# A two-layer squared-ReLU MLP: smaller first loads, a shorter warm-up and a reordered tail

## The chip, the cores and the metric

The kernel runs on one core of a Trainium2 chip. The metric is device time in microseconds (us), the median of several executions. The kernel before was measured again beside each set of experiments, on the same chip. The profile's span is counted from its first to its last instruction and is about 1.7 us shorter than the measured time.

## The reference, cut to what matters

```python
B, S, D, F = 1, 2048, 640, 1536           # bf16 everywhere
h = jnp.einsum("bsd,df->bsf", x, w1) + b1
r = jnp.where(h > 0, h, 0)
h = r * r
out = jnp.einsum("bsf,fd->bsd", h, w2) + b2
```

## The kernel before

Rows of x are handled in 16 tiles of 128. The kernel gives x to TensorE transposed. Tiles 0 to 3 are loaded plainly and transposed on TensorE; tiles 4 to 15 come transposed by DMA later. The first product (x times w1) is made in 48 groups of five 128x512 matmuls; the first two groups are cut into four 128-column parts ("S1s"), so that a part can start when its own x tile is there. ScalarE applies bias and ReLU, VectorE squares. The second product (h times w2) is made per x tile in a wide half (512 columns, "A") and a narrow one (128 columns, "B"); VectorE adds b2 to each.

The order of work on TensorE ("T" is the transpose of one x tile):

```python
    N_WARM = 8
    sched = [("T", 0), ("T", 1),
             ("S1s", 0, 0), ("S1s", 0, 1), ("T", 2), ("S1s", 1, 0), ("S1s", 1, 1), ("T", 3), ("b1T",),
             ("S1s", 0, 2), ("S1s", 1, 2), ("S1s", 0, 3), ("S1s", 1, 3)]
    for g in range(N_SPLIT_G, NG):
        sched.append(("S1", g))
    # ...
    for tc in range(NTC):
        sched.append(("S2", tc))
    W1_PIECES = [(0, 2), (2, 4), (4, 8), (8, 12)]
    X_LOADS = [(0, 2), (2, 3), (3, 4)]
```

The loads of the head. A "w1 piece" is some 128-column blocks of w1; piece 0 has what the two first groups need.

```python
        @block.sync
        def _(sp):
            dma_x(sp, 0, 2)          # x tiles 0 and 1 in one load, 320 KB
            dma_x(sp, 2, 3)
            dma_x(sp, 3, 4)
            dma_w1(sp, 1)
            dma_w1(sp, 2)
            dma_w1(sp, 3)
            # ... waits, then transposing loads of x, then w2, then the stores
        @block.scalar
        def _(act):
            dma_w1(act, 0)           # w1 piece 0, 320 KB, from ScalarE's own queue
            act.wait_ge(sem_tiny, 1)
            act.activation(tiny_sb[:, 4:8], tiny_sb[:, 0:4], ACTF.Relu)   # fetches the table early (1.28 us, from 1.33 in the trace)
```

TensorE's warm-up, on constants, while nothing has arrived yet:

```python
            for i in range(N_WARM):
                pe.matmul(bank_f32(BANK_WARM), wlhs, wmov, start=True, stop=True)   # 128x512
```

## Time and profile before

| | before |
|---|---|
| time, median of 3 runs | 114.68 us (114.59 to 114.92) |
| span of the profiled run | 112.8 us |
| TensorE (PE) busy | 109.3 us, 97% |
| first transposes / first "S1s" matmuls / 128x512 matmuls start | 4.43 / 5.42 / 8.45 us |
| TensorE's end / last add's end / last store landed | 110.41 / 110.74 / 112.44 us |

These lines are from the profile page of the kernel before: the span, the busy time of each engine, and the chain of work that ended last, as shares of the span by engine and by line.

```profile
span 112.8 us, 1645 instructions
PE 109.3 (97%) x683; PEld 56.5 (50%) x683; DVE 49.6 (44%) x85; ACT 36.2 (32%) x55; POOL 1.9 (2%) x8
...
PE 96%; DVE 1%; ACT 0%; issue 0%
PE psum L375 44%; PE psum L393 37%; PE psum L406 9%; PE psum L314 3%; PE psum L357 2%; PE psum L341 1%; DVE o_sb L301 1%; ACT xT_sb L170 0%; DVE o_sb L305 0%; PE psum L327 0%
...
w_sb<-in_w_dram ACTq DMA_DIRECT2D x1, 320.0 KB, 4.4
```

L375 and L393 are the 128x512 matmuls of the two products: 81% of the span. The last line says that w1 piece 0, issued by ScalarE, landed 4.4 us after its issue. The next lines are the chain of the kernel before in order of time (start in us, length in us, what): its head.

```profile
0.85 3.57 PE psum L314 x8
4.42 0.01 issue
4.43 0.34 PE psum L341 x3
...
4.80 0.49 ACT xT_sb L170
5.28 0.14 issue
5.42 0.74 PE psum L357 x10
...
8.61 1.51 PE psum L375 x7
```

The warm-up (L314) fills the time until x lands (x tiles 0 and 1: 4.30 us). Its matmuls start 427 ns apart; those of the same 128x512 shape later, at full clock, start 216 ns apart. Then come transposes (L341), a copy on ScalarE, and at 5.42 the first product. From there TensorE has no gap. A gain can only come from the part before 5.42 us or from the tail. The tail, from the timeline of the kernel before (start, length, engine, line, out<-in, count, idle time before it and what ended that):

```profile
109.58 0.83 PE L406 MATMUL psum<-w_sb,h2T_sb 128*128 128x128 bf16 x12
...
109.78 0.69 DVE L301 TENSOR_TENSOR o_sb<-psum,b_sb 128x512 bf16<-128x512 f32 x1 [2.30 <-PE psum L393]
110.45 0.29 DVE L305 TENSOR_TENSOR o_sb<-psum,b_sb 128x128 bf16<-128x128 f32 x1
110.50 0.36 ACTq L272 DMA_DIRECT2D out_dram<-o_sb  x1
110.77 0.33 SPq L223 DMA_DIRECT2D out_dram<-o_sb  x1
```

The last wide add and the last narrow matmuls end together, the narrow add follows, and two stores (128 KB and 32 KB) are issued within 0.3 us of each other.

### The profile page before, as it was taken

The numbers are of one execution on the slowest core, as the hardware profiler recorded it, in microseconds if no ns is written. First come the engines' busy times: TensorE is split into PE (matmuls) and PEld (weight loads), VectorE is DVE, ScalarE is ACT, GpSimd is POOL, SyncE is SP. The second block draws the span as 40 slices with busy tenths as digits, with TensorE's granted clock in tenths as the row PEclk, the third lists the DMA queues.
The fourth block names the chain that finished last, engine by engine and source line by source line (L and its number), as shares of the span: only waits on it lengthen the run. The fifth ranks groups of instructions, "written<-read, shape, count | busy, mean of one in ns | idle before, by whom it ended". The sixth has DMA issues, their size and how long they took to land.

```text
span 112.8 us, 1645 instructions
## 1 busy us (share of the span) xinstructions
PE 109.3 (97%) x683; PEld 56.5 (50%) x683; DVE 49.6 (44%) x85; ACT 36.2 (32%) x55; POOL 1.9 (2%) x8
## 2 busy tenths in 40 slices
PE   7999999999999999999999999999999999999991
PEld 2494444444444444444445554555555455555550
DVE  0227667566575665766655212333331133333212
ACT  5338575665756656657560000000000000000000
POOL 4000000002000000000000000000000000000000
PEclk9999999999999999999999999999999999999999
DMA  2997649285980000000000111110111111011111
GB/s 72 315 329 220 139 94 218 55 191 150 360 301 2 9 0 0 0 0 0 0 0 0 67 58 58 58 52 6 64 58 58 58 58 58 25 39 58 58 58 58
DMA packets 15143, 9.61 MB, mean 85 GB/s; under 512 B 8352, under 2 KB 15008, under 8 KB 15136
## 3 DMA queue, kind: packets, MB, share of 16 engines
q1 hardware_dynamic: 14160, 8.72, 26.8%
q10 hardware_dynamic: 800, 0.46, 1.3%
q0 software_dynamic: 176, 0.33, 1.0%
q8 instruction: 5, 0.08, 0.3%
q14 instruction: 2, 0.02, 0.1%
HBM read 4.75 MB, written 2.62 MB: 65 GB/s over the span
## 4 chain that ended last, share of the span: by engine, by line
PE 96%; DVE 1%; ACT 0%; issue 0%
PE psum L375 44%; PE psum L393 37%; PE psum L406 9%; PE psum L314 3%; PE psum L357 2%; PE psum L341 1%; DVE o_sb L301 1%; ACT xT_sb L170 0%; DVE o_sb L305 0%; PE psum L327 0%
## 5 line engine op out<-in xcount | busy, mean ns | idle before, releaser
L375 PE MATMUL psum<-xT_sb,w_sb 128*128 128x512 bf16 x230 | 49.8, 379 | 0.0
L393 PE MATMUL psum<-w_sb,h2T_sb 128*128 128x512 bf16 x192 | 44.0, 379 | 0.0
L281 DVE TENSOR_TENSOR h2T_sb<-r_sb 128x512 bf16<-128x512 f32 x48 | 33.1, 692 | 19.0 <-ACT r_sb L251 19.0
L251 ACT ACTIVATE r_sb<-psum,b_sb 128x512 f32<-128x512 f32 x48 | 32.9, 687 | 18.4 <-PE psum L375 17.7
L375 PEld LDWEIGHTS psum<-xT_sb,w_sb 128*128 128x128 bf16 x230 | 22.5, 98 | 26.9
L393 PEld LDWEIGHTS psum<-w_sb,h2T_sb 128*128 128x128 bf16 x192 | 18.2, 98 | 19.1
L301 DVE TENSOR_TENSOR o_sb<-psum,b_sb 128x512 bf16<-128x512 f32 x16 | 11.1, 691 | 35.7 <-PE psum L393 35.7
L406 PEld LDWEIGHTS psum<-w_sb,h2T_sb 128*128 128x128 bf16 x192 | 12.1, 98 | 3.8
L406 PE MATMUL psum<-w_sb,h2T_sb 128*128 128x128 bf16 x192 | 13.3, 219 | 0.0
L305 DVE TENSOR_TENSOR o_sb<-psum,b_sb 128x128 bf16<-128x128 f32 x16 | 4.6, 291 | 0.0
L314 PE MATMUL psum<-const-bfloat16-1.0 128*128 128x512 bf16 x8 | 3.6, 628 | 0.8 <-PEq L424 0.8
L172 DVE COPY xT_sb<-psum 128x256 bf16<-128x256 bf16 x4 | 1.2, 292 | 5.5 <-PE psum L341 5.5
L357 PE MATMUL psum<-xT_sb,w_sb 128*128 128x128 bf16 x40 | 2.8, 219 | 0.3 <-ACT xT_sb L170 0.3
L170 ACT COPY xT_sb<-psum 128x384 bf16<-128x384 bf16 x4 | 1.8, 480 | 3.0 <-PE psum L341 3.0
L357 PEld LDWEIGHTS psum<-xT_sb,w_sb 128*128 128x128 bf16 x40 | 2.3, 98 | 0.5 <-DMA w_sb<-in_w_dram 0.4
L314 PEld LDWEIGHTS psum<-const-bfloat16-1.0 128*128 128x128 bf16 x8 | 1.0, 139 | 2.5 <-issue 2.5
L242 ACT ACT_TABLE_LOAD x1 | 1.3, 1283 | 1.3 <-PEq L424 1.3
L341 PEld LDWEIGHTS psum<-id_sb,x_sb 128*128 128x128 bf16 x20 | 1.2, 97 | 0.9 <-issue 0.9
L341 PE MATMUL psum<-id_sb,x_sb 128*128 128x128 bf16 x20 | 1.6, 219 | 0.0
L236 POOL DMA_DIRECT2D b_sb<-in_b_dram x1 | 0.6, 566 | 23.5 <-DMA xT_sb<-in_x_dram 23.5
L234 POOL DMA_DIRECT2D b1row_sb<-in_b_dram x1 | 0.7, 678 | 0.1
L276 DVE MEMSET tiny_sb<- 128x8 f32 x1 | 0.1, 65 | 0.9 <-PEq L424 0.9
(10 smaller groups left out, 1.5 us busy)
## 6 DMA issues: line engine op xcount, KB each, us to landing
out_dram<-o_sb SPq DMA_DIRECT2D x15, 160.0 KB, 1.8
w_sb<-in_w_dram SPq DMA_DIRECT2D x1, 1920.0 KB, 9.1
w_sb<-in_w_dram SPq DMA_DIRECT2D x2, 640.0 KB, 7.0
x_sb<-in_x_dram SPq DMA_DIRECT2D x1, 320.0 KB, 3.5
w_sb<-in_w_dram ACTq DMA_DIRECT2D x1, 320.0 KB, 4.4
x_sb<-in_x_dram SPq DMA_DIRECT2D x2, 160.0 KB, 4.3
w_sb<-in_w_dram SPq DMA_DIRECT2D x1, 320.0 KB, 5.0
b_sb<-in_b_dram POOLq DMA_DIRECT2D x1, 320.0 KB, 7.1
```

The lines of the kernel that those rows point to most:

```text
L170: eng.copy(dst, src).then_inc(sem_xTa, 1)
L242: act.activation(tiny_sb[:, 4:8], tiny_sb[:, 0:4], ACTF.Relu)
L251: act.activation(r_sb[:, g % R, :], bank_f32(BANK_S1[g % 4]), ACTF.Relu, bias=b1_sb[:, fc:fc + 1], scale=1.0,).then_inc(sem_R, 1)
L281: dve.tensor_tensor(h2T_sb[:, fc, ts * TS:(ts + 1) * TS], r_sb[:, g % R, :], r_sb[:, g % R, :], ALU.mult,).then_inc(sem_H, 1)
L301: dve.tensor_tensor(o_sb[:, tc, 0:DA], bank_f32(BANK_S2A[tc % 3]), b2_sb[:, 0:DA], ALU.add,).then_inc(sem_OA, 1)
L305: dve.tensor_tensor(o_sb[:, tc, DA:D], bank_f32(BANK_S2B[tc % 2], DB), b2_sb[:, DA:D], ALU.add,).then_inc(sem_OB, 1)
L314: pe.matmul(bank_f32(BANK_WARM), wlhs, wmov, start=True, stop=True)
L341: ins = pe.transpose(dst, x_sb[:, tc, dc * P:(dc + 1) * P], id_sb[:, :])
L357: ins = pe.matmul(bank_f32(BANK_S1[g % 4])[:, tc * P:(tc + 1) * P], w1_sb[:, dc, fc * P:(fc + 1) * P], xT_sb[:, dc, tc * P:(tc + 1) * P], ...
L375: ins = pe.matmul(bank_f32(BANK_S1[g % 4]), w1_sb[:, dc, fc * P:(fc + 1) * P], xT_sb[:, dc, ts * TS:(ts + 1) * TS], start=(dc == 0), stop= ...
L393: ins = pe.matmul(bank_f32(bA), h2T_sb[:, fc, tc * P:(tc + 1) * P], w2_sb[:, fc, 0:DA], start=(fc == 0), stop=(fc == NFC - 1),)
L406: ins = pe.matmul(bank_f32(bB, DB), h2T_sb[:, fc, tc * P:(tc + 1) * P], w2_sb[:, fc, DA:D], start=(fc == 0), stop=(fc == NFC - 1),)
```

## The change

The intent: tile 0 of x should arrive alone and early, so that the transposes can start earlier and two warm-up matmuls can go; one matmul ("W") is put after the transposes, where TensorE waits for w1. w1 piece 0 moves from ScalarE's queue to SP's, behind x tiles 0 and 1. At the end, the last two tiles do their wide halves first and their narrow halves last, so that the wide add and its store overlap the narrow matmuls.

```diff
-    N_WARM = 8
+    N_WARM = 6
-    sched = [("T", 0), ("T", 1),
+    sched = [("T", 0), ("T", 1), ("W", 1),
              ("S1s", 0, 0), ("S1s", 0, 1), ("T", 2), ...
-    for tc in range(NTC):
+    for tc in range(NTC - 2):
         sched.append(("S2", tc))
+    sched += [("S2A", NTC - 2), ("S2A", NTC - 1), ("S2B", NTC - 2), ("S2B", NTC - 1)]
-    X_LOADS = [(0, 2), (2, 3), (3, 4)]
+    X_LOADS = [(0, 1), (1, 2), (2, 3), (3, 4)]
 ... on SP:
-            dma_x(sp, 0, 2)
+            dma_x(sp, 0, 1)
+            dma_x(sp, 1, 2)
+            dma_w1(sp, 0)
             dma_x(sp, 2, 3)
             dma_x(sp, 3, 4)
             dma_w1(sp, 1)
 ... the store of tile 14 is cut in two (A and B); 18 stores instead of 17
 ... on ScalarE:
-            dma_w1(act, 0)
             act.wait_ge(sem_tiny, 1)
 ... VectorE and TensorE handle "S2A" and "S2B" apart; unused names are removed
```

More of the change, by code (lines that the diff above doesn't have):

```diff
@@ L108, in bass_standalone__dense_activation_squared_relu__prompt_kernel @@
         ones_sb = sb("ones_sb", [P, P], BF16)
-        zero_sb = sb("zero_sb", [P, P], BF16)
         tiny_sb = sb("tiny_sb", [P, 8], F32)
@@ L135, in bass_standalone__dense_activation_squared_relu__prompt_kernel @@
         sem_ones = sem("ones")
-        sem_zero = sem("zero")
         sem_tiny = sem("tiny")
@@ L147, in wait_evac @@
             eng.wait_ge(sem_xTa if e == "act" else sem_xTd, n)
-        def wait_evac_all_upto(eng, tc):
-            na = max([n for (t, _p), (e, n) in evac_count.items() if e == "act" and t_order.index(t) <= t_order.index(tc)], default=0)
-            nd = max([n for (t, _p), (e, n) in evac_count.items() if e == "dve" and t_order.index(t) <= t_order.index(tc)], default=0)
-            if na:
-                eng.wait_ge(sem_xTa, na)
-            if nd:
-                eng.wait_ge(sem_xTd, nd)
         def emit_evac(eng_name, eng, tc, part):
@@ L195, in dma_w1 @@
             eng.dma_start(w1_sb[:, :, lo * P:hi * P], src).then_inc(sem_w1[i], 16)
-        n_out_dmas = NTC + 1
+        n_out_dmas = NTC + 2
         @block.sync
         def _(sp):
-            dma_x(sp, 0, 2)
+            dma_x(sp, 0, 1)
+            dma_x(sp, 1, 2)
+            dma_w1(sp, 0)
             dma_x(sp, 2, 3)
@@ L216, in _ @@
             sp.dma_start(w2_sb[:, :, :], src).then_inc(sem_w2, 16)
-            for tc in range(NTC):
-                if tc < NTC - 1:
-                    sp.wait_ge(sem_OB, tc + 1)
-                    sp.dma_start(out2[tc * P:(tc + 1) * P, :], o_sb[:, tc, :]).then_inc(sem_out, 16)
-                else:
-                    sp.wait_ge(sem_OB, tc + 1)
-                    sp.dma_start(out2[tc * P:(tc + 1) * P, DA:D], o_sb[:, tc, DA:D]).then_inc(sem_out, 16)
+            for tc in range(NTC - 2):
+                sp.wait_ge(sem_OB, tc + 1)
+                sp.dma_start(out2[tc * P:(tc + 1) * P, :], o_sb[:, tc, :]).then_inc(sem_out, 16)
+            tc = NTC - 2
+            sp.wait_ge(sem_OA, tc + 1)
+            sp.dma_start(out2[tc * P:(tc + 1) * P, 0:DA], o_sb[:, tc, 0:DA]).then_inc(sem_out, 16)
+            for tc in (NTC - 2, NTC - 1):
+                sp.wait_ge(sem_OB, tc + 1)
+                sp.dma_start(out2[tc * P:(tc + 1) * P, DA:D], o_sb[:, tc, DA:D]).then_inc(sem_out, 16)
             sp.wait_ge(sem_out, 16 * n_out_dmas)
@@ L295, in _ @@
                     square(item[1])
-                elif kind == "S2":
+                elif kind in ("S2", "S2A", "S2B"):
                     tc = item[1]
-                    if tc == 0:
-                        dve.wait_ge(sem_b2, 16)
-                    dve.wait_ge(sem_S2A, tc + 1)
-                    dve.tensor_tensor(
-                        o_sb[:, tc, 0:DA], bank_f32(BANK_S2A[tc % 3]), b2_sb[:, 0:DA], ALU.add,
-                    ).then_inc(sem_OA, 1)
-                    dve.wait_ge(sem_S2B, tc + 1)
-                    dve.tensor_tensor(
-                        o_sb[:, tc, DA:D], bank_f32(BANK_S2B[tc % 2], DB), b2_sb[:, DA:D], ALU.add,
-                    ).then_inc(sem_OB, 1)
+                    if kind in ("S2", "S2A"):
+                        if tc == 0:
+                            dve.wait_ge(sem_b2, 16)
+                        dve.wait_ge(sem_S2A, tc + 1)
+                        dve.tensor_tensor(
+                            o_sb[:, tc, 0:DA], bank_f32(BANK_S2A[tc % 3]), b2_sb[:, 0:DA], ALU.add,
+                        ).then_inc(sem_OA, 1)
+                    if kind in ("S2", "S2B"):
+                        dve.wait_ge(sem_S2B, tc + 1)
+                        dve.tensor_tensor(
+                            o_sb[:, tc, DA:D], bank_f32(BANK_S2B[tc % 2], DB), b2_sb[:, DA:D], ALU.add,
+                        ).then_inc(sem_OB, 1)
         @block.tensor
@@ L324, in _ @@
                 kind = item[0]
-                if kind == "b1T":
+                if kind == "W":
+                    for i in range(item[1]):
+                        pe.matmul(bank_f32(BANK_WARM), wlhs, wmov, start=True, stop=True)
+                elif kind == "b1T":
                     pe.wait_ge(sem_b1row, 16)
@@ L379, in _ @@
                     ins.then_inc(sem_S1, 1)
-                elif kind == "S2":
+                elif kind in ("S2", "S2A", "S2B"):
                     tc = item[1]
                     ts = tc // TPS
-                    pe.wait_ge(sem_H, NFC * (ts + 1))
-                    if tc == 0:
-                        pe.wait_ge(sem_w2, 16)
-                    bA = BANK_S2A[tc % 3]
-                    if tc < 3:
-                        g_last = max(g for g in range(NG) if BANK_S1[g % 4] == bA)
-                        pe.wait_ge(sem_R, g_last + 1)
-                    else:
-                        pe.wait_ge(sem_OA, tc - 3 + 1)
-                    for fc in range(NFC):
-                        ins = pe.matmul(
-                            bank_f32(bA), h2T_sb[:, fc, tc * P:(tc + 1) * P], w2_sb[:, fc, 0:DA],
-                            start=(fc == 0), stop=(fc == NFC - 1),
-                        )
-                    ins.then_inc(sem_S2A, 1)
+                    if kind in ("S2", "S2A"):
+                        pe.wait_ge(sem_H, NFC * (ts + 1))
+                        if tc == 0:
+                            pe.wait_ge(sem_w2, 16)
+                        bA = BANK_S2A[tc % 3]
+                        if tc < 3:
+                            g_last = max(g for g in range(NG) if BANK_S1[g % 4] == bA)
+                            pe.wait_ge(sem_R, g_last + 1)
+                        else:
+                            pe.wait_ge(sem_OA, tc - 3 + 1)
+                        for fc in range(NFC):
+                            ins = pe.matmul(
+                                bank_f32(bA), h2T_sb[:, fc, tc * P:(tc + 1) * P], w2_sb[:, fc, 0:DA],
+                                start=(fc == 0), stop=(fc == NFC - 1),
+                            )
+                        ins.then_inc(sem_S2A, 1)
+                    if kind == "S2A":
+                        continue
                     bB = BANK_S2B[tc % 2]
```

## The prediction

> **What bounds the kernel now.** TensorE. The page's first part gives PE 109.3 of 112.8 us busy (97%); the chain of waits puts 96% of the span on PE, 81% of it in two lines that the change leaves alone: the 128x512 matmuls of the first product (49.6 us, 230 of them, 216 ns apart) and of the second (16 groups of 2.59 us). From 8.61 to 110.4 us the chain has no gap. So only the head (0 to 8.6 us) and the tail (after 110.4 us) can give anything.
>
> **Head before** (timeline and chain). Warm-up: 8 matmuls start 427 ns apart, 0.85 to 4.42 us. The first x load (320 KB, 3.5 us from issue to landing) lands at 4.3 us, so the warm-up just covers it. Transposes 4.43 to 5.15; then PE waits until 5.42, for ScalarE's first copy (4.80 to 5.28) and the first w1 piece (issued 0.81, landing 4.4 us later; the weight load waited for it until 5.39). Ten first-product matmuls take 0.74 us where 10 x 56 ns would do (the second copy ends at 5.66). The big matmuls start at 8.45.
>
> **Head after.**
> - x tile 0 alone is half the bytes: from the packet record (x packets begin at 1.9 us, about 256 KB per us, the semaphore some 0.5 us later) I estimate landing at 3.3, tile 1 at 3.9 us.
> - Two warm-up matmuls fewer: 0.85 us less, end near 3.5. Both tiles are transposed 3.5 to 4.5, partly at half speed (107 ns each). [...] (matmuls 427 ns apart from 0.85, transposes 55 ns apart at 4.43; clock record full from 4.35). I expect full speed near 4.3 again. The extra matmul (0.21 to 0.43 us) fits into the wait.
> - The w1 piece moves from ScalarE's queue to third on SP's: issue 0.9 us later, but it need not share with x. [...] (the two queues' packets interleave from 2.9 to 3.8 us). The bytes ahead of it are the same 320 KB, so it lands about as before: 5.0 (before 5.2).
> - First-product matmuls start at about 5.05 instead of 5.42, and the 0.18 us stall among the first ten goes. The later x tiles land at about 5.3 and 5.8, in time.
> Gain in the head: 0.3 to 0.5 us, all on the critical path, since PE is gapless afterwards.
>
> **Tail.** PE does the same 24 + 24 matmuls and ends at the same point. Before, the last 128x512 add (0.69 us) ends at 110.47, the last 128x128 add (0.29) at 110.74, its store issues at 110.77, landing 1.7 us later. After, the large add runs 0.67 us earlier, but the last narrow matmul still ends at 110.41, then 0.29 us of add, then the same store. Worth at most 0.05 us.
>
> **Predicted:** 114.25 us (from 114.68), range 113.8 to 114.8. Faster by over 2%: 0.02; within 2%: 0.95; slower: 0.03.
>
> **What would show it.** First transposes near 3.5; first-product matmuls from 5.05; big matmuls about 0.4 us earlier; last narrow add within 0.35 us of PE's end.
>
> **What would make it wrong.** The clock rising late, because fewer real matmuls fill the warm-up[...]: matmuls would start 107 ns apart beyond 5 us and up to 1 us would be lost. Or the w1 piece landing after 5.5.

114.68 us, less 0.3 to 0.5 us in the head and at most 0.05 us in the tail, came to 114.25. Two steps stand as my estimates: full speed near 4.3 us, from the one trace of the kernel before (4.35 us), and piece 0 at 5.0 us, from the 320 KB ahead of it and the interleaved packets of that trace.

## The result, and the profile after

| | before | after |
|---|---|---|
| time, median | 114.74 us (114.57 to 114.92, 14 runs) | 114.89 us (114.36 to 116.83, 12 runs) |
| span of the profiled run | 112.8 | 113.2 |
| first transposes start | 4.43 | 3.36 |
| first "S1s" matmuls start | 5.42 | 5.98 |
| 128x512 matmuls start | 8.45 | 8.99 |
| last add ends to last store landed | 1.70 | 1.47 |

The ratio of the fast runs is 1.0007 with a 95% interval of 0.9993 to 1.0021. A ratio here is the mean time of one kernel's fast runs over the mean of the other's fast runs of the same rounds, so it is not quite the ratio of the medians. The result is "the same", a little above the range that I gave (113.8 to 114.8). Executions over 1.5% slower than the fastest of the same kernel are left out of the means. Two of the 12 runs took 116.26 and 116.83 us; they are not in the ratio. The kernel before has no such run.

From the page of the changed kernel, the lines that answer to those shown of before:

```profile
span 113.2 us, 1645 instructions
PE 108.8 (96%) x682; PEld 56.7 (50%) x682; DVE 49.7 (44%) x85; ACT 36.3 (32%) x55; POOL 1.9 (2%) x8
...
PE 93%; DMA 4%; SPq 1%; DVE 0%; issue 0%
PE psum L374 44%; PE psum L393 37%; PE psum L408 9%; DMA w_sb<-in_w_dram 4%; PE psum L356 2%; SPq L181 1%; PE psum L340 0%; DVE o_sb L301 0%; PE psum L326 0%
```

A load of w1 stands in the chain now, where there was none. The head of the chain in order of time, changed kernel:

```profile
1.72 4.21 DMA w_sb<-in_w_dram
5.93 0.05 issue
5.98 0.73 PE psum L356 x10
...
9.16 0.86 PE psum L374 x4
```

The warm-up, the transposes and the copy have left the chain. They were done early: the timeline of the changed kernel has

```profile
3.36 1.12 PE L340 MATMUL psum<-id_sb,x_sb 128*128 128x128 bf16 x10
3.92 0.97 ACT L161 COPY xT_sb<-psum 128x384 bf16<-128x384 bf16 x2 [1.61 <-PE psum L340]
...
4.32 0.38 PE L323 MATMUL psum<-const-bfloat16-1.0 128*128 128x512 bf16 x1
...
5.98 0.73 PE L356 MATMUL psum<-xT_sb,w_sb 128*128 128x128 bf16 x10 [1.28 <-DMA w_sb<-in_w_dram]
```

so the second copy ends at 4.89 us, and TensorE, done with its extra matmul at 4.70, stands for 1.28 us until w1 piece 0 has landed (5.93 us). I had expected 5.0. Full clock came at nearly the same time in the two profiles (4.35 and 4.20 us; in the changed kernel the starts of the transposes go from 107 ns apart to 56 there), so the clock does not part their heads. The tail of the changed kernel:

```profile
109.45 1.50 PE L408 MATMUL psum<-w_sb,h2T_sb 128*128 128x128 bf16 x24
...
109.66 0.69 DVE L296 TENSOR_TENSOR o_sb<-psum,b_sb 128x512 bf16<-128x512 f32 x1 [1.90 <-PE psum L393]
110.33 0.29 DVE L301 TENSOR_TENSOR o_sb<-psum,b_sb 128x128 bf16<-128x128 f32 x1
110.38 0.38 ACTq L266 DMA_DIRECT2D out_dram<-o_sb  x1
110.64 1.00 SPq L218 DMA_DIRECT2D out_dram<-o_sb  x2
111.00 0.29 DVE L301 TENSOR_TENSOR o_sb<-psum,b_sb 128x128 bf16<-128x128 f32 x1 [0.38 <-PE psum L408]
```

The last add still follows TensorE's end directly, as predicted. But its store now has more time to itself: by the trace's record the last store landed 1.47 us after the last add's end (112.76 after 111.29) instead of 1.70 us (112.44 after 110.74).

The sum: head 0.54 us later (8.45 to 8.99), tail about 0.22 us shorter, together 0.32 us, which is the difference of the two profiled runs (114.88 against 114.56).

### The profile page after: what moved, and what is told of

Its sections match the earlier page's. It is cut to its first block, busy times and chain, and to the rows that moved or that the text cites. A ratio compares the mean times of both kernels' runs of the same rounds, so it can differ in the third digit from the quotient of the medians.

```text
span 113.2 us, 1645 instructions
## 1 busy us (share of the span) xinstructions
PE 108.8 (96%) x682; PEld 56.7 (50%) x682; DVE 49.7 (44%) x85; ACT 36.3 (32%) x55; POOL 1.9 (2%) x8
## 3 DMA queue, kind: packets, MB, share of 16 engines
HBM read 4.75 MB, written 2.62 MB: 65 GB/s over the span
## 4 chain that ended last, share of the span: by engine, by line
PE 93%; DMA 4%; SPq 1%; DVE 0%; issue 0%
PE psum L374 44%; PE psum L393 37%; PE psum L408 9%; DMA w_sb<-in_w_dram 4%; PE psum L356 2%; SPq L181 1%; PE psum L340 0%; DVE o_sb L301 0%; PE psum L326 0%
## 5 line engine op out<-in xcount | busy, mean ns | idle before, releaser
L310 PE MATMUL psum<-const-bfloat16-1.0 128*128 128x512 bf16 x6 | 2.7, 624 | 0.8 <-PEq L426 0.8
L340 PEld LDWEIGHTS psum<-id_sb,x_sb 128*128 128x128 bf16 x20 | 1.7, 118 | 0.6 <-issue 0.6
```

Of the source, the lines that this page charges most:

```text
L340: ins = pe.transpose(dst, x_sb[:, tc, dc * P:(dc + 1) * P], id_sb[:, :])
```

## The experiments

Two things needed a cause: why w1 piece 0 lands so late, and why some runs take over 116 us. The theories:

- **A**: the place of the piece on SP's queue makes it land late and unevenly. Its rivals: **B**, the split of x does it; **C**, chance; **D**, the number of loads queued on SP does it.
- **W**: six warm-up matmuls are too little activity in some executions, and the clock is granted one period later (in the profile of e1 full clock came at 8.53 us and lasted 105.813 us, 3.413 us less than the 109.226 us of the kernel before). Its rival **M**: the slow runs come from stalls of the loads.

How evenly a load lands can be read from the trace: it records each increment of a load's semaphore, and has 16 of them for each load. Those of w1 piece 0 came from 4.54 to 5.93 us in the changed kernel. "Spread" below is the time from the first to the last of them. The kernel makes TensorE wait for all 16: in the changed kernel the first product began at 5.98 us, 0.05 us after the last increment and 0.99 us after the 12th. The expectations say "engine" for what brings an increment; that each comes from one DMA engine was not shown. For w1 piece 0:

| kernel (one profile each) | where piece 0 is issued | 12th of 16 | landed | spread |
|---|---|---|---|---|
| before | ScalarE, first | 5.03 | 5.17 | 0.41 |
| e2, e6, e13 (x not split) | ScalarE, first | 5.09 to 5.21 | 5.23 to 5.39 | 0.48 to 0.57 |
| e1, e4, e7, e12 (x split) | ScalarE, first | 4.26 to 4.52 | 4.46 to 4.69 | 0.32 to 0.52 |
| e3, e11 (x not split) | SP, second | 4.63, 4.80 | 5.08, 5.04 | 0.78, 0.51 |
| e14 (x split) | SP, second | 4.33 | 4.50 | 0.56 |
| after, e8, e5 (x split) | SP, third | 4.99, 4.88, 5.37 | 5.93, 6.21, 6.00 | 1.39, 1.57, 1.25 |
| e9, e10 (x split, fewer behind it) | SP, third | 5.12, 5.05 | 5.61, 5.60 | 0.97, 1.09 |

### e1: piece 0 back on ScalarE's queue

```diff
 changed kernel, on SP:
-            dma_w1(sp, 0)
 on ScalarE:
+            dma_w1(act, 0)
             act.wait_ge(sem_tiny, 1)
```

> The changed kernel with one part undone: the first w1 piece is issued again from ScalarE's queue. Theory A (the move of the w1 piece to third place on SP's queue makes it land late and unevenly): it lands near 5.1 us again with about 0.4 us between its first and last engine (changed kernel: 5.93, with 1.39 us between them), big matmuls begin at 8.0 to 8.3 us, time 113.9 to 114.3, runs tight within 0.4 us. Theory B (four smaller x loads do it): the piece still lands after 5.6, time about 114.8. Theory C (chance stalls of the memory in that one execution): spread over 1 us between runs in any kernel, the one before too.

Piece 0 landed at 4.46 us with a spread of 0.43, even with x split: theory B falls. But the time was no better, 116.05 us median (7 runs from 114.50 to 116.79; four at 116 and above), ratio of those counted as fast 0.9985 (0.9964 to 1.0005). The timeline of this run says why:

```profile
4.94 0.71 PE L340 MATMUL psum<-id_sb,x_sb 128*128 128x128 bf16 x5 [0.85 <-DMA x_sb<-in_x_dram]
...
5.88 1.27 PE L356 MATMUL psum<-xT_sb,w_sb 128*128 128x128 bf16 x10
```

First, x tile 1 landed at 4.90 us (3.59 in the changed kernel): w1 piece 0, issued at 0.81 us on the other queue, went ahead of tile 1, issued at 1.27. That is a reason to move the piece behind tile 1. Second, ten matmuls took 1.27 us here and 0.73 us in the changed kernel: this run, which is counted as fast, ran at half speed (107 ns from one of these matmuls to the next instead of 56) until 8.53 us, where the clock record begins to show full speed. My times for this run were wrong on both counts.

### e2: the tail alone

```diff
 kernel before:
-    for tc in range(NTC):
+    for tc in range(NTC - 2):
         sched.append(("S2", tc))
+    sched += [("S2A", NTC - 2), ("S2A", NTC - 1), ("S2B", NTC - 2), ("S2B", NTC - 1)]
     (and the stores and handlers of the change that belong to it)
```

> The kernel before with the new tail order alone. From the two traces I read that the tail gave 0.22 us (last store landing 1.47 us after the last add against 1.69). If that is the reorder, this runs 0.15 to 0.3 us faster than before (114.45 to 114.6), head unchanged. As I predicted it: at most 0.05 us.

Median 114.52 us against 114.77, ratio 0.9986 (0.9969 to 1.0004). The last store landed 1.51 us after the last add. The trace shows the 0.2 us; the interval of the times still touches 1. (The head of this one profile was slower than before, with the same code: its transposes took 1.12 us instead of 0.72 and the first product began at 5.64 instead of 5.42 us, as full clock came at 5.38 instead of 4.35 us. Single profiles differ by such tenths.)

### e3: only the move of piece 0 to SP, x not split

```diff
 kernel before, on SP:
             dma_x(sp, 0, 2)
+            dma_w1(sp, 0)
 on ScalarE:
-            dma_w1(act, 0)
```

> The kernel before with only the w1 piece moved to SP's queue, behind the first (unsplit) x load. Theory A: the piece lands after 5.6 us, with over 1 us between its first and last engine, time 115.0 to 115.6, runs spread by over 0.5 us. Theory B: as before, 114.7 within 0.15, spread of the landing 0.4 us.

Theory A missed here. The spread grew to 0.78 us, but the piece landed at 5.08 us, and the first product began at 5.19 us, earlier than before. The head of the chain:

```profile
1.30 3.77 DMA w_sb<-in_w_dram
5.08 0.12 issue
5.19 0.75 PE psum L357 x10
```

Median 114.62 against 114.77, ratio 0.9995 (0.9975 to 1.0016). Here the piece stands second, and the move did not delay it. But x tiles 2 and 3 behind it came in with spreads of 0.95 and 1.23 us, where the kernel before had 0.42 and 0.43.

### e4: only the split of x

```diff
 kernel before:
-    X_LOADS = [(0, 2), (2, 3), (3, 4)]
+    X_LOADS = [(0, 1), (1, 2), (2, 3), (3, 4)]
-            dma_x(sp, 0, 2)
+            dma_x(sp, 0, 1)
+            dma_x(sp, 1, 2)
```

> The kernel before with only the x load of two tiles split in two. Theory A: the w1 piece lands near 5.2 as before, with 0.4 us between engines; no gain either, since the eight warm-up matmuls last until 4.4 us: 114.5 to 114.75. Theory B: landing after 5.6, 115.0 or more, runs spread.

The piece landed at 4.50 us with a spread of 0.52, so B is out again. Tile 1 again went behind it and landed at 4.98. Median 114.89 against 114.77, ratio 1.0010 (0.9994 to 1.0027): alone the split is worth nothing.

### e5: the changed kernel with eight warm-up matmuls

```diff
-    N_WARM = 6
+    N_WARM = 8
```

> The changed kernel with eight warm-up matmuls again (the extra one after the transposes stays). Theory W (with six warm-up matmuls the activity before the wait for w1 is too thin, so in some executions the clock is granted one period of 3.4 us later): no run above 115.4 us, median 114.4 to 114.8. Theory M (the slow runs come from the stalls of the loads): runs above 116 appear here too, as in the changed kernel.

Six runs from 114.60 to 115.09 us, median 115.00, ratio 1.0010 (0.9989 to 1.0030): no slow run, as theory W has it, though with 2 slow ones in 18 of the changed kernel six runs alone would say little. The median was 0.2 us above my range; piece 0 landed late here too (6.00).

### e6: the kernel before with six warm-up matmuls

```diff
-    N_WARM = 8
+    N_WARM = 6
```

> The kernel before with six warm-up matmuls and nothing else. Theory W: runs of 116 to 117 us appear among fast ones near 114.7, in two groups; the loads are as before, 0.4 us between a piece's first and last engine. Theory M: as before, all within 114.5 to 115.

Two groups: 114.82 and 114.83, and 115.87, 116.05, 116.32 and 116.87 us. The loads of its profile are nearly as before (spreads of 0.52 to 0.63 us). One number in the kernel before makes the slow runs, without any change of the loads: theory M is not needed. (The profile fell on a fast run, so the clock of the slow ones was not seen here.) The median is 115.96, ratio 1.0067 (1.0021 to 1.0112), in which three of the four slow ones count as fast by the rule of 1.5%.

### e7: piece 0 on ScalarE's queue, meant to be later

```diff
 changed kernel, on SP:
-            dma_w1(sp, 0)
 on ScalarE:
             act.activation(tiny_sb[:, 4:8], tiny_sb[:, 0:4], ACTF.Relu)
+            dma_w1(act, 0)
```

> The changed kernel with the first w1 piece on ScalarE's queue again, but behind its table load, at about 2.3 us, so that it cannot go ahead of x tile 1 (in the run where it went to that queue first, tile 1 landed at 4.9 instead of 3.8 us). Theory A: tile 1 lands near 3.8, the w1 piece by 5.3 with about 0.4 us between engines; first-product matmuls from 5.3 if full clock. Theory D (the pieces come in unevenly because there are more loads queued on SP, eight instead of six, whichever they are): the w1 piece lands evenly, and the last w1 piece still has over 0.6 us between engines. With six warm-up matmuls theory W expects some runs near 116 to 117.

The edit did not do what I wanted: the issue went out at 0.98 us, while the table load (0.81 to 2.09) was still running, and ahead of tile 1's issue at 1.26 (tile 1 landed at 5.03; in the changed kernel at 3.59, not the 3.8 of my expectation). As a test of place it repeats e1: landed 4.69 us, spread 0.44. Times 114.51, 114.69, 114.80, 116.26, 116.48 and 116.74. Its profile fell on a slow run (116.48) and shows the late clock:

```profile
6.01 1.27 PE L356 MATMUL psum<-xT_sb,w_sb 128*128 128x128 bf16 x10
...
7.61 1.27 PE L356 MATMUL psum<-xT_sb,w_sb 128*128 128x128 bf16 x10
...
9.47 0.73 PE L356 MATMUL psum<-xT_sb,w_sb 128*128 128x128 bf16 x10
```

Ten matmuls take 1.27 us until the clock record begins at 9.47 us, and 0.73 us from there.

### e8: the changed kernel once more

No edit.

> The changed kernel once more, unchanged, for a second profile and more runs. If the uneven landing belongs to the change, the first w1 piece again has over 1 us between its first and last engine and lands after 5.6 us; if it was chance, it has 0.4 to 0.6 us and lands by 5.2. Times: most between 114.4 and 115.2, one in four to six above 116.

Piece 0 landed at 6.21 us with a spread of 1.57: theory C falls for it. Six runs, 114.74 to 115.39, median 114.98; no slow one this time, so 2 of 18 runs of the changed kernel in all.

### e9 and e10: fewer loads queued behind piece 0

```diff
 changed kernel, on SP, e9:
+            sp.wait_ge(sem_x[1], 16)
             dma_w1(sp, 1)
 e10 instead:
+            sp.wait_ge(sem_w1[0], 16)
             dma_w1(sp, 1)
```

> The changed kernel, with SP waiting until x tile 1 has landed (3.6 to 3.8 us) before it issues the other three w1 pieces. Theory D (what is queued behind on SP makes the engines of the first w1 piece drift apart): the piece comes in with at most 0.7 us between its engines and lands by 5.3 us, fast runs at 114.2 to 114.5. Theory A (its place on SP's queue among the x tiles does it): spread still above 1 us, landing after 5.7, 114.8 to 115.2 as the changed kernel.

> The same, but SP waits for the first w1 piece itself, so that at most five loads are ever queued before it lands. Theory D: spread of at most 0.6 us, landing by 5.1; first-product matmuls from 5.1 us; the second w1 piece lands by 8.0, just in time or 0.3 us late, so 114.2 to 114.7. Theory A: spread above 1 us, landing after 5.7, and later pieces late, 115.2 or more.

Neither theory met its numbers. Piece 0 landed at 5.61 and 5.60 us, 0.3 to 0.6 us earlier than in the three runs with all loads queued, but with a spread of about 1.0 us. In e10 the second piece then came late, as this part of its chain shows:

```profile
1.73 3.87 DMA w_sb<-in_w_dram
...
5.62 3.26 DMA w_sb<-in_w_dram
8.88 0.27 issue
9.15 1.03 PE psum L375 x4
```

Medians 115.21 and 115.04 against 114.91, ratios 1.0025 (0.9990 to 1.0060) and 1.0016 (0.9987 to 1.0044). What is queued behind seems to have a part in it, but the smaller one; this rests on one profile each. In e9 the unevenness began one load earlier: x tile 1 landed at 4.24 us with a spread of 0.92.

### e11: the tail and the move of piece 0, without the rest

```diff
 kernel before with the tail of e2 and the two DMA lines of e3
```

> The kernel before with the new tail and the first w1 piece second on SP's queue (x not split, eight warm-up matmuls). In its own run the w1 move let the first-product matmuls begin at 5.19 instead of 5.42 us; the tail gave about 0.2. If both add: 114.2 to 114.45, no run above 115.2, ratio 0.996 to 0.998.

Median 114.61 against 114.91 us, ratio 0.9970 (0.9946 to 0.9994), six runs from 114.07 to 114.89. It beats the kernel before by 0.3%. The absolute time was above my range; the kernel before ran 0.17 us slower in this set. Its one profile (114.70 us) does not show the head's gain: the first product began at 5.40 us, at first at half speed (full clock at 5.66), and TensorE then waited for x tile 2, which landed at 6.27 with a spread of 1.27. So how much of the 0.3% is the head's stays open.

### e13 and e14: the number alone, the place alone

```diff
 e13, kernel before (eight loads on SP, the early ones as before):
-    W1_PIECES = [(0, 2), (2, 4), (4, 8), (8, 12)]
+    W1_PIECES = [(0, 2), (2, 4), (4, 6), (6, 8), (8, 10), (10, 12)]
 (and two more dma_w1 lines)

 e14, changed kernel (the same eight loads, two exchanged):
-            dma_x(sp, 1, 2)
             dma_w1(sp, 0)
+            dma_x(sp, 1, 2)
```

> The kernel before with its last two w1 pieces cut in two, so that eight loads instead of six are queued on SP, the early ones as before. Theory D (the number of loads queued on SP): the last pieces drift to over 0.8 us between their engines (before: 0.37 to 0.42). Theory A (place of the first piece, small loads ahead of it): all stay within 0.6 us. The first product starts at 5.4 us either way, time as before within 0.2.

> The changed kernel with the first w1 piece second on SP's queue instead of third: x tile 0, w1, x tile 1, the same eight loads. Theory A (place): at most 0.8 us between the engines of the w1 piece, landing by 4.9 us; then x tile 1 is the late one, at 5.1 or later. Theory D (number queued): still over 1 us between its engines, landing after 5.4. Time in either case 114.7 to 115.2, with some runs above 116, because tile 1 comes late and the activity is thin.

e13: all spreads stayed within 0.47 and 0.59 us; theory D, as I had put it, falls. There is one reserve: the trace has SP's five issues of the w1 pieces stretched over 4.75 us (2.28 to 7.03; three took 1.57 us in the kernel before), so SP itself was held back and fewer loads may really have been queued. Median 114.82, ratio 0.9982 (0.9956 to 1.0009).

e14: with the same eight loads, piece 0 in second place landed at 4.50 us with a spread of 0.56. It stood behind 160 KB less. At the 331 GB/s that the kernel before moved between 5.42 and 8.6 us, 160 KB take about 0.5 us (an estimate from that rate), but the piece landed 1.43 to 1.71 us earlier; the rest is the unevenness. Behind it, x tiles 2 and 3 were uneven in its place (1.26 and 1.34). Tile 1 was then late:

```profile
1.71 3.23 DMA x_sb<-in_x_dram
4.94 0.05 issue
4.99 0.45 PE psum L340 x5
```

Four runs, 114.70 to 116.13, one slow; ratio 1.0015 (0.9969 to 1.0060).

### e12: a version that uses the early tile

If piece 0 is issued first on ScalarE's queue, it lands before tile 1. So TensorE should not wait for tile 1 at all, but multiply tile 0 at once.

```diff
 e1, plus:
-    sched = [("T", 0), ("T", 1), ("W", 1),
-             ("S1s", 0, 0), ("S1s", 0, 1), ("T", 2), ("S1s", 1, 0), ("S1s", 1, 1), ("T", 3), ("b1T",),
+    sched = [("T", 0), ("W", 1), ("S1s", 0, 0), ("S1s", 1, 0),
+             ("T", 1), ("T", 2), ("S1s", 0, 1), ("S1s", 1, 1), ("T", 3), ("b1T",),
```

> A version meant to beat both: the changed kernel with the first w1 piece first on ScalarE's queue (it landed at 4.46 us there, ahead of x tile 1 at 4.90), and TensorE takes the two first-product groups of x tile 0 before it transposes tile 1. Work from the head: first-product matmuls from 4.5 us instead of 5.42, no wait of over 0.3 us after that, TensorE busy almost without a gap from 0.84 us[...]: big matmuls from 7.6 to 8.0 us, time 113.7 to 114.2, no run above 115.2. If theory W is wrong and six warm-up matmuls are bad in themselves, runs above 116 appear.

Median 114.44 us against 114.90, six runs from 114.12 to 114.75, ratio 0.9949 (0.9922 to 0.9976): 0.5% faster than before, and the lowest ratio of all kernels here, though its interval overlaps those of e2 and e11. There is no slow run with its six warm-up matmuls. From its timeline:

```profile
4.66 0.73 PE L356 MATMUL psum<-xT_sb,w_sb 128*128 128x128 bf16 x10
5.23 0.80 PE L340 MATMUL psum<-id_sb,x_sb 128*128 128x128 bf16 x10
...
6.13 0.73 PE L356 MATMUL psum<-xT_sb,w_sb 128*128 128x128 bf16 x10
...
8.81 4.48 PE L374 MATMUL psum<-xT_sb,w_sb 128*128 128x512 bf16 x20 [0.34 <-DMA w_sb<-in_w_dram]
```

The first product began at 4.66 us (I expected 4.5). It missed its range because the second w1 piece landed at 8.54 us in this run and TensorE waited for it until 8.81: 15 of its 16 increments had come by 7.05 us, and the last came alone at 8.54. In each of the next two loads, too, one increment came 1.4 to 1.5 us after the other 15.

## Why the prediction was wrong, point by point

**The step that failed: "The bytes ahead of it are the same 320 KB, so it lands about as before: 5.0 (before 5.2)."** It landed at 5.93 us, and at 6.00 and 6.21 in the two other profiles of this order. Three quarters of its increments had come by about the expected time, at 4.99 us in the profiled run. But the kernel waits for all 16, and in third place on SP's queue, with all loads queued, the first and the last were 1.25 to 1.57 us apart, against 0.3 to 0.8 for piece 0 in every other place. So the first product began at 5.98 us and not at 5.05, and the gain of 0.3 to 0.5 us in the head became a loss of 0.54 us in the profiled run. Its place decided whether piece 0 was hit: one exchange (e14) took it from third to second and to 4.50 us. But third place is not bad in itself: with piece 0 on ScalarE's queue (e1, e4, e7, e12) the third load on SP's, x tile 2, had a spread of 0.30 to 0.53. What parts the traces cleanly is the queue. In all eight profiles with piece 0 on SP's queue, piece 0 or one of the x tiles has a spread of 0.97 to 1.57; in the eight with it on ScalarE's queue none of them is over 0.6. e1 and e3 change this alone, in opposite directions, and agree. The move also changes when the loads are issued, and no run parts the two. The loads behind piece 0 may have a smaller part (e9, e10: 5.60). What makes some increments come late is not settled. It is not the number of loads alone (e13; and e1 and e3 both have seven loads on SP's queue, with spreads of up to 0.51 and 1.23 among these early ones), not the split (e4) and not chance (five of five profiles with the piece in third place have a spread above 0.9). Later loads on SP are uneven by chance as well: with the same list of loads on SP the second w1 piece had a spread of 0.49 us in e1 and 1.80 in e12. The largest in the changed kernel was 2.37 us, of the third w1 piece.

**The rival that I named came true in some runs.** I had written that the clock might rise late because fewer real matmuls fill the warm-up, at a cost of up to 1 us. Two of 18 runs were slow, by about 1.4 and 2 us (116.26 and 116.83 against 114.88). Neither was profiled; that the clock came late in them is inferred from e1 and e7, whose profiles show it in runs 1.4 and 1.8 us slower than the median fast run of the same kernel (116.05 against 114.64, 116.48 against 114.69: 1.2 and 1.6%). In the profiles that have the clock record (e4 has none), the time at full clock is 109.226 us, but 105.813 us in the two where it came late (e1, e7). The two differ by 3.413 us, and are 32 and 31 times that. So I take 3.413 us as a period at whose end the clock is granted or not; this is an estimate from these figures. The start of the full clock differed from run to run: 4.35 us in the kernel before, 3.82 to 6.08 us in other fast runs (3.0 to 5.2 us after the first matmul at 0.84). In the late ones it was 8.53 and 9.47 us, so that by this reading one period had ended without a grant at 5.12 and 6.06 us. In both of these, TensorE had stood for 0.85 and 0.98 us in that period, waiting for tile 1. By the number of warm-up matmuls, counting runs of 115.8 us and above:

| | slow runs |
|---|---|
| eight: the kernel before (58 runs), e2, e3, e4, e5, e11, e13 (34 runs) | 0 |
| six, gap (1.28 us or more) only after both transposes: after and e8 | 2 of 18 |
| six, gap (0.85 us or more) earlier, before the transposes of tile 0 or tile 1: e1, e6, e7, e14 | 12 of 23 |
| six, loads held back: e9, e10 | 0 of 12 |
| six, no such gap: e12 | 0 of 6 |

Two runs of e9 (115.69 and 115.77) lie just under the line and cannot be put in either group. e6 shows with one number changed that the shorter warm-up makes slow runs. It is the warm-up and the gap behind it together, as e12 has six and no slow run in the six that I have. The traces also show how busy TensorE was in these periods. In the 3.41 us just before full clock TensorE was busy for at least 2.72 us in every profile with the record (least in e6, from 0.41 to 3.82 us; 2.83 in e10); in the two periods that went by without a grant it was busy for 2.57 (e1) and 2.44 us (e7). If busy time is what decides, which no run here tests, I estimate from these that the line lies between 2.57 and 2.72 us. The chance in it would fit: by this reading, with a gap, the same work passes or fails by where the period happens to begin.

**"The 0.18 us stall among the first ten goes": there was none.** The chain gave 0.74 us for the ten matmuls, and I compared it with 10 x 56 ns. The next transposes started at 6.00 us, 0.58 us after the first of the ten; the rest of the 0.74 is the end of the last matmul, which overlaps what follows (one is recorded as 0.22 us long, at starts 56 ns apart). The changed kernel shows 0.73 for the same group, with the copies long done.

**The tail, "worth at most 0.05 us", was mis-sized.** The mechanism that I saw was right: the last add still follows TensorE's end. But I took the store's 1.7 us as fixed. Before, a 128 KB store was issued only 0.27 us ahead of the last 32 KB store; now it goes out 0.9 us ahead, and from the last add to the last landing it takes 1.47 us instead of 1.70 (1.51 in e2). That is 0.2 us. That the two stores had got in each other's way is my reading, and the semaphore record supports it: before, the 32 increments of the two stores came as one run without a break, from 112.06 to 112.44 us, 12 ns apart; after, the last store's 16 came alone, from 112.58 to 112.76. No run parts the stores by itself. The times agree with it (e2: 0.9986) but do not prove it alone.

**Right:** TensorE bounds the kernel, and only head and tail can move; tiles 0 and 1 landed at 3.16 and 3.59 us (predicted 3.3 and 3.9), the first transposes started at 3.36 (near 3.5), partly at half speed (107 ns apart, then 56); the clock came at 4.20 in the profiled run (near 4.3); the change stays within 2%. So the early x tiles arrived as planned, and had nothing to be multiplied with.

## What to carry to other kernels

When a load gates the start, look at when its last increment comes, not at the bytes ahead of it: one exchange in the queue changed that by 1.4 us or more with the same loads. Do not trim a warm-up to what the loads just cover: run it often enough to see the two groups of times (e6: 114.8, and 115.9 to 116.9), and leave no gap behind it (e12: no slow run in six). Bringing one operand early paid here only where the order of work used it before the other operands came (e12: 0.9949; e4: 1.0010).
